# A gated recurrence followed by a highway layer: the identity taken from the raw w_h on GpSimd, w_t scaled on ScalarE, and a new hand-written order of the work

## The chip, the core and the metric

The kernel runs on one core of one Trainium2 chip. The metric is the device time of one execution in microseconds (us); the median of three executions of the kernel before is 207.73 us (207.66 to 208.34). The engines are PE (TensorE: transposes and matrix products), DVE (VectorE), ACT (ScalarE), POOL (GpSimd) and SP (SyncE, which issues the DMAs of this kernel).

## What is computed

`x` and `f_logit` are (4, 6336, 256) in float32, `lower_bound` has 256 entries, `w_h` and `w_t` are 256 by 256 and `b_t` has 256 entries.

```python
sig = 1 / (1 + exp(-f_logit))
f = lower_bound + (1 - lower_bound) * sig
i = 1 - f
for t in range(S):                       # each batch starts from h = 0
    h = f[:, t] * h + i[:, t] * x[:, t]
    y[:, t] = h
H = maximum(y @ w_h, 0)
T = 1 / (1 + exp(-(y @ w_t + b_t)))
out = T * H + (1 - T) * y
```

With c = 1 - lower_bound and u = sigmoid(-f_logit), f is 1 - c u and i is c u. The kernel leaves c out of the recurrence: it scans y' = f y' + u x, so y = c y', and puts c into the weights and into the diagonal that carries y to the output. Since out = y + T (max(y w_h, 0) - y), and max(a, 0) - y = max(a - y, -y), the kernel subtracts the identity from `w_h` once, and one DVE instruction gives the maximum.

## The kernel before

The 25344 tokens are cut into 21 units, listed in `parts` (line 42): units 0 and 1 have 2 blocks of 128 tokens, unit 2 has 4, units 3 to 6 and 14 to 18 have 8, units 7 to 13 have two halves of 8, units 19 and 20 have 4 and 2. A half is called a sub-unit.

The whole order is written out by hand as a string of tokens (lines 49 to 109). A loop at the end (line 414) reads the tokens one after another and calls the function of that letter; every instruction is pinned to that order on its engine, so each engine works through its own tokens in the order of the string and waits where an operand isn't there yet. A token is a letter, the unit, sometimes the sub-unit and a half, and after the colon the buffer or the PSUM banks. A trailing `v` puts the token on DVE instead of its usual engine.

The letters of one unit, in the order in which they depend on each other:

- `l`, `x` (SP, line 250): load f_logit and x. `u` (ACT, line 262): u = sigmoid(-l) in float16.
- `b`, `B` (POOL, or DVE with `v`, line 277): the product u x, as half a sub-unit (`b`) or a whole one (`B`). For 8 blocks `b` has 1024 elements in each partition, `B` 2048.
- `i`, `p` (PE, lines 286 and 311): transpose u and the product into PSUM, for feature half 0 or 1. `f` (ACT or DVE, lines 301 and 299): f from the transposed u.
- `s` (DVE, line 320): the recurrence along the tokens of one feature half. Each `s` of a unit starts from the last column of the unit before, so the scans of one feature half form a chain through the kernel.
- `z`, `g` (PE, lines 333 and 145): the two matrix products with `w_t` and `w_h`. `t` (ACT, line 356): the sigmoid of z. `d` (DVE, line 363): the maximum of g and -y. `e`, `E` (POOL or DVE, line 377): d times t, for one feature half or both.
- `o` (PE, lines 393 and 394): y times the diagonal plus the product, transposed back to tokens. `c` (ACT or DVE, lines 405 and 403): PSUM to SBUF. `w` (SP, line 411): the store.

`k*n` are n matrix products of zeros that nobody reads; there are 49 of them, all in the first part. Where DVE and POOL both multiply two SBUF tensors, the helper `shared` (line 193) makes the next POOL product wait for the last such DVE product.

Six tokens without a unit prepare constants. `wt` and `wh` (SP) load the two weights, `cc` (DVE) makes c, -c and the bias, `dg` (DVE, lines 219 and 220) a float16 diagonal of c and a float32 diagonal of -c, `WT` (DVE, line 224) scales w_t by c, and `WH` (DVE, lines 230 and 232) scales w_h by c and adds the negative diagonal to the two square blocks that hold the identity. All of them stand in the first 12 us.

Two queues set much of the order around the change. SP issues loads and stores in one line, and a store waits there for its `c`, so the loads behind it wait too. PE works through its tokens in one line as well; a `p` that waits for a product holds every later `z`, `g` and `o`.

Of the kernel before, what the change touches and what calls it, by code (L numbers as in the profile page):

```python
# [54 lines left out]
g2.0.0:1 d2.0.0:2 z2.0.0:0 t2.0.0:2 g2.0.1:3 k*1:2 o0.0.0:2 p3.0.1:0 l5.0:0 u4.0:0 z2.0.1:4 t2.0.1 e2.0.0 x5.0:0
b4.0.0:1 o1.0.0:1 p3.0.0:5 k*4:6 s3.1:0 l6.0:1 c0.0.0:0 x6.0:1 i4.0.1:4 f4.1:0 b4.0.1 k*4:0 k*4:0 s3.0:1 i4.0.0:0
l7.1:2 g3.0.1:67 d2.0.1 e2.0.1 c1.0.0v:1 w1.0.0 d3.0.1:3 u5.0:1 i5.0.1:2 p4.0.0:1 B5.0:2 i5.0.0:3 z3.0.0:45 f4.0:3
f5.1:2 f5.0:1 g3.0.0:67 z3.0.1:23 t3.0.0:0 w0.0.0 x7.1:2 s4.0:2 p4.0.1:0 p5.0.0:1 o2.0.0:45 u6.0:2 d3.0.0 e3.0.0
l7.0:3 t3.0.1 x7.0:3 c2.0.0:2 i6.0.1:6 f6.1:3 s4.1:3 g4.0.1:23 p5.0.1:0 u7.1:3 e3.0.1v d4.0.1:0 o3.0.1:45 c3.0.1:3
z4.0.1:67 t4.0.1:1 o3.0.0:23 z4.0.0:45 s5.0:4 i6.0.0:1 b6.0.1:0 c3.0.0:1 t4.0.0 g4.0.0:67 s5.1:5 g5.0.1:23 d4.0.0  # L60
b6.0.0 p6.0.0:0 z5.0.1:67 l8.0:4 f6.0:0 u7.0:0 t5.0.1:2 w3.0.1 l8.1:0 b7.1.1:1 x8.1:4 d5.0.1:1 z5.0.0:45 s6.0:0 t5.0.0
i7.0.1:23 i7.1.1 f7.1:1 b7.1.0 e4.0.1 e4.0.0v p6.0.1:1 s6.1:1 w2.0.0 g5.0.0:67 x8.0:0 o4.0.0:45 c4.0.0:0 g6.0.1:23
u8.0:1 l9.1:1 o4.0.1:45 p7.1.1:01 d5.0.0 b7.0.0:2 d6.0.1:2 c4.0.1:3 b7.0.1 p7.0.1 l9.0:2 e5.0.0v i7.0.0:67 e5.0.1
w3.0.0 u8.1:2 i7.1.0 s7.1:2 f7.0:2 p7.0.0:45 p7.1.0 z6.0.0:23 x9.0:1 z6.0.1:67 t6.0.0:0 t6.0.1 i8.0.1:01 s7.0:3 i8.1.1
i8.0.0:23 w4.0.0 g6.0.0:67 x9.1:2 d6.0.0 f8.1:0 i8.1.0 f8.0:3 o5.0.0:01 c5.0.0:2 g7.0.0:45 d7.0.0:3 u9.0:0 g7.1.1:23
d7.1.1:0 B8.1:0 p8.1.1:67 u9.1:3 g7.0.1:01 d7.0.1 o5.0.1:45 c5.0.1:1 B8.0:2 p8.0.1 s8.1:4 z7.0.1:23 t7.0.1:1 z7.1.1:01
w4.0.1 z7.0.0:45 t7.1.1:2 t7.0.0 p8.1.0:23 p8.0.0 E6.0 o6.0.1:01 c6.0.1:0 o6.0.0:67 c6.0.0:3 b9.0.0:1 z7.1.0:45
i9.0.0:01 b9.0.1 i9.1.0 b9.1.0:0 g7.1.0:67 t7.1.0 b9.1.1 l10.1:3 s8.0:5 l10.0:4 f9.0:1 i9.1.1:45 e7.0.1 u10.1:2 w5.0.1
d7.1.0 e7.0.0 g8.1.1:23 d8.1.1:1 x10.1:3 g8.1.0:01 d8.1.0 i9.0.1 f9.1:2 w5.0.0 g8.0.0:67 p9.1.1:23 p9.0.1 i10.1.0:01
# [111 lines left out]

# [270 lines left out]
```

## Time and profile before

| | us |
|---|---|
| median of three executions | 207.73 |
| the profiled execution | 208.83 |
| its span, first to last instruction | 207.1 |
| busy: PE, DVE, ACT, POOL | 194.7, 192.8, 190.9, 171.9 |
| first scan of unit 3 starts | 20.56 |
| first scan of unit 4 starts | 28.19 |
| last scan (unit 20) ends | 199.00 |
| last PSUM copy ends | 204.10 |

The profiled execution takes 1.73 us more than its span. The page lists for each engine how long it was busy; the views behind it list each instruction with its start, its duration, and in brackets the idle time of its engine before it with what ended that idle time. Durations of neighbours on DVE overlap a little: the start of the next lies some hundredths to a tenth of a microsecond before the end of the one before.

### The profile page before, as it was taken

To read this page: it belongs to the slowest core of one execution; us is meant where nothing else is said; L and a number is where in the kernel's file an instruction comes from. 1 tells how busy PE (TensorE), PEld (TensorE's weight loads), DVE (VectorE), ACT (ScalarE), POOL (GpSimd) and SP (SyncE) were. 2 spreads that over 40 slices of the span, in tenths; PEclk is the share of its full clock that TensorE was granted. 3 is DMA by queue.
4 is the path that set the end of the run, shared out by engine and by line. 5 is a ranking of instruction groups with operands and counts; after the bars stand their busy time and mean duration, and the time that the engine had idled before them with its cause. 6 is when DMAs were issued, how large, how long until landed. Compare 5 with 4: busy or idle time off the path is not lost.

```text
span 207.1 us, 4606 instructions
## 1 busy us (share of the span) xinstructions
PE 194.7 (94%) x1850; PEld 135.0 (65%) x1850; DVE 192.8 (93%) x141; ACT 190.9 (92%) x173; POOL 171.9 (83%) x90
## 2 busy tenths in 40 slices
PE   7999988998799999999989999999999999999991
PEld 2566657556566858747846967658767587677780
DVE  2799989999999999999999979999999999999971
ACT  4479699999999999999998999999999999998792
POOL 3173798978999999978998899979979949999920
PEclk9999999999999999999999999999999999999999
DMA  6999999999999999999999999999999999934576
GB/s 178 365 425 416 418 423 418 418 419 412 425 418 420 420 419 421 424 417 419 427 415 418 423 414 429 418 417 427 412 424 390 403 325 352 364 141 161 206 304 253
DMA packets 15980, 78.67 MB, mean 380 GB/s; under 512 B 1748, under 2 KB 2264, under 8 KB 10072
## 3 DMA queue, kind: packets, MB, share of 16 engines
q1 hardware_dynamic: 15952, 78.39, 93.5%
q8 instruction: 14, 0.23, 0.5%
q14 instruction: 6, 0.05, 0.1%
q10 hardware_dynamic: 8, 0.00, 0.0%
HBM read 52.43 MB, written 25.95 MB: 379 GB/s over the span
## 4 chain that ended last, share of the span: by engine, by line
PE 48%; DVE 17%; ACT 16%; DMA 11%; issue 4%; POOL 2%; SPq 1%; DVEq 0%; ACTq 0%
PE psum L333 13%; PE psum L145 11%; DMA l<-in_f_logit_dram 11%; DVE y L320 10%; PE psum L393 6%; DVE d L363 6%; PE psum L394 6%; ACT f L301 6%; PE psum L286 6%; PE psum L311 5%; ACT u L262 4%; ACT t L356 3%; ACT o L405 2%; POOL bv L277 2%; DVE f L299 1%
## 5 line engine op out<-in xcount | busy, mean ns | idle before, releaser
L277 POOL TENSOR_TENSOR bv<-u,x 128x1024 bf16<-128x1024 f16 (+2 forms) x44 | 99.8, 2293 | 18.3 <-ACT f L301 7.4
L320 DVE TENSOR_TENSOR_SCAN y<-f,y,psum 128x1024 bf16<-128x1024 f16 (+6 forms) x40 | 103.7, 2614 | 1.0 <-ACT f L301 0.6
L377 POOL TENSOR_TENSOR d<-d,t 128x1024 bf16<-128x1024 bf16 (+3 forms) x35 | 71.7, 2063 | 11.4 <-ACT t L356 6.1
L333 PE MATMUL psum<-y,w_sb 128*128 128x512 bf16 (+1 forms) x224 | 77.4, 367 | 3.0 <-ACT f L301 1.9
L145 PE MATMUL psum<-y,w_sb 128*128 128x512 bf16 x184 | 69.7, 379 | 0.7 <-DVE y L320 0.7
L363 DVE SCALAR_TENSOR_TENSOR d<-y,ncc,psum 128x1024 bf16<-128x1024 bf16 (+2 forms) x56 | 62.6, 1147 | 3.4 <-PE psum L145 1.5
L356 ACT ACTIVATE t<-psum,bt 128x1024 bf16<-128x1024 f32 (+2 forms) x56 | 56.3, 1038 | 2.6 <-PE psum L145 1.7
L262 ACT ACTIVATE u<-l 128x2048 f16<-128x2048 f32 (+2 forms) x28 | 48.6, 1747 | 5.4 <-DMA l<-in_f_logit_dram 5.4
L301 ACT ACTIVATE f<-psum,ncc 128x1024 f16<-128x1024 f16 (+3 forms) x38 | 50.9, 1365 | 1.6 <-PE psum L286 1.6
L405 ACT COPY o<-psum 128x1024 f32<-128x1024 f32 (+1 forms) x49 | 48.5, 1031 | 2.2 <-PE psum L394 1.0
L393 PE MATMUL psum<-diag,y 128*128 128x128 f16 x396 | 48.8, 219 | 0.6 <-ACT f L301 0.4
L394 PE MATMUL psum<-ident_b,d 128*128 128x128 bf16 x396 | 48.6, 219 | 0.8 <-DVE d L377 0.8
L394 PEld LDWEIGHTS <-d 128*128 128x128 bf16 x396 | 44.0, 113 | 4.8 <-DVE d L377 1.2
L393 PEld LDWEIGHTS <-y 128*128 128x128 bf16 x396 | 44.2, 113 | 2.5
L333 PEld LDWEIGHTS <-w_sb 128*128 128x128 f16 x224 | 21.6, 98 | 18.1 <-issue 1.0
L145 PEld LDWEIGHTS <-w_sb 128*128 128x128 f16 x184 | 17.9, 97 | 21.3 <-issue 6.0
L311 PE MATMUL psum<-ident_f,bv 128*128 128x128 f32 x198 | 29.3, 276 | 1.3 <-POOL bv L277 0.8
L286 PE MATMUL psum<-ident_h,u 128*128 128x128 f16 x396 | 28.6, 219 | 1.2 <-ACT u L262 0.8
L286 PEld LDWEIGHTS <-u 128*128 128x128 f16 x396 | 25.0, 98 | 6.9 <-ACT u L262 2.1
L311 PEld LDWEIGHTS psum<-ident_f,bv 128*128 128x128 f32 x198 | 22.4, 141 | 7.1 <-POOL bv L277 2.1
L377 DVE TENSOR_TENSOR d<-d,t 128x1024 bf16<-128x1024 bf16 (+3 forms) x15 | 10.6, 718 | 0.2
L145 PE MATMUL psum<-zeros 128*128 128x512 bf16 x39 | 10.6, 399 | 0.0
(33 smaller groups left out, 38.6 us busy)
## 6 DMA issues: line engine op xcount, KB each, us to landing
out_dram<-o SPq DMA_DIRECT2D x48, 512.0 KB, 7.9
l<-in_f_logit_dram SPq DMA_DIRECT2D x23, 1024.0 KB, 14.6
x<-in_x_dram SPq DMA_DIRECT2D x23, 1024.0 KB, 14.4
l<-in_f_logit_dram SPq DMA_DIRECT2D x2, 512.0 KB, 5.9
x<-in_x_dram SPq DMA_DIRECT2D x2, 512.0 KB, 7.4
l<-in_f_logit_dram SPq DMA_DIRECT2D x3, 256.0 KB, 3.7
x<-in_x_dram SPq DMA_DIRECT2D x3, 256.0 KB, 5.5
out_dram<-o SPq DMA_DIRECT2D x3, 256.0 KB, 5.6
```

The source lines that it names most:

```text
L145: return pe.add_instruction(mybir.InstMatmult(name=nc.get_next_instruction_name(), start_tensor_calc=start, stop_tensor_calc=stop, tile_si ...
L277: shared(pin(e.tensor_mul(st[n]["bv", s][:, a:c].rearrange("p k d j -> p k j d"), st[n]["u", s][:, 2 * a:2 * c].rearrange("p (k j) d -> p ...
L286: pin(nc.tensor.transpose(uT[:, j * P:(j + 1) * P], st[n]["u", s][:, j, h * P:(h + 1) * P], ident_h))
L301: pin(nc.scalar.activation(to, of, AF.Identity, scale=ncc[:, h:h + 1], bias=1.0))
L311: pin(nc.tensor.transpose(words[:, k:k + g * (P - 1) + 1:g], pair, ident_f))
L320: pin(nc.vector.tensor_tensor_scan(y[:, c:e], st[n]["f", h][:, c:e], data, 0.0 if fresh else carry[h], op0=ALU.mult, op1=ALU.add))
L333: pin(nc.tensor.matmul(p.part(a, e), w, data, start=ki == 0, stop=ki == NH - 1))
L356: pin(nc.scalar.activation(half(n, q, "t", m), z, AF.Sigmoid, bias=bt[:, m:m + 1]))
L363: pin(nc.vector.scalar_tensor_tensor(half(n, q, "d", m), y, ncc[:, m:m + 1], g, op0=ALU.mult, op1=ALU.max))
L377: shared(pin(e.tensor_mul(d, d, t)), not eng)
L393: pin(nc.tensor.matmul(o, st[n]["y", h][:, whole], diag[:, h], start=True, stop=False))
L394: pin(nc.tensor.matmul(o, half(n, q, "d", h)[:, cols], ident_b, start=False, stop=True))
```

## The change

There are two parts. The first concerns the constants. `WI`, a new token, subtracts the float32 identity from the two square blocks of the raw `w_h`, in place, on POOL. After it `WH` is two plain scalings on DVE (`WHv`), and `WT` becomes two scalings on ACT. `dg` makes only the diagonal of c; `ndiag` is gone. The constants' functions now take an engine.

```
-    ndiag = sb([P, NH, P], FP32, "ndiag")
...
-    def do_dg(slot):
+    def do_dg(slot, eng):
         for h in range(NH):
-            pin(nc.vector.tensor_scalar(diag[:, h], ident_h, cc[:, h:h + 1], None, op0=ALU.mult))
-            pin(nc.vector.tensor_scalar(ndiag[:, h], ident_h, ncc[:, h:h + 1], None, op0=ALU.mult))
-
-    def do_WT(slot):
+            if eng:
+                pin(nc.vector.tensor_scalar(diag[:, h], ident_h, cc[:, h:h + 1], None, op0=ALU.mult))
+            else:
+                pin(nc.gpsimd.tensor_scalar(diag[:, h], ident_h, cc[:, h:h + 1], None, op0=ALU.mult))
+
+    def do_WI(slot, eng):
+        e = nc.vector if eng else nc.gpsimd
         for h in range(NH):
-            pin(nc.vector.tensor_scalar(w_sb[:, 1, h], w_raw[:, 1, h], cc[:, h:h + 1], None, op0=ALU.mult))
-
-    def do_WH(slot):
+            own = w_raw[:, 0, h, h * P:(h + 1) * P]
+            shared(pin(e.tensor_tensor(own, own, ident_f, op=ALU.subtract)), not eng)
+
+    def scaled(k, eng):
         for h in range(NH):
-            own = slice(h * P, (h + 1) * P)
-            rest = slice((1 - h) * P, (2 - h) * P)
-            pin(nc.vector.scalar_tensor_tensor(w_sb[:, 0, h, own], w_raw[:, 0, h, own], cc[:, h:h + 1], ndiag[:, h],
-                                               op0=ALU.mult, op1=ALU.add))
-            pin(nc.vector.tensor_scalar(w_sb[:, 0, h, rest], w_raw[:, 0, h, rest], cc[:, h:h + 1], None,
-                                               op0=ALU.mult))
+            if eng:
+                pin(nc.vector.tensor_scalar(w_sb[:, k, h], w_raw[:, k, h], cc[:, h:h + 1], None, op0=ALU.mult))
+            else:
+                pin(nc.scalar.mul(w_sb[:, k, h], w_raw[:, k, h], cc[:, h:h + 1]))
+
+    def do_WT(slot, eng):
+        scaled(1, eng)
+
+    def do_WH(slot, eng):
+        scaled(0, eng)
```

The second part is the order: the whole string is replaced, and with it some choices of engine. Its first line before and after:

```
-l0.0:0 u0.0:0 pc:0 k*4:1 x0.0:0 b0.0.0v:0 p0.0.0:1 i0.0.1:2 cc dg f0.1v:0 p0.0.1:0 i0.0.0:3 l1.0:1 u1.0:1 l2.0:2
+pc:0 cc k*4:1 l1.0:0 l0.0:1 u1.0:0 u0.0:1 i0.0.0:0 x0.0:0 b0.0.0v:0 x1.0:1 b1.0.0v:1 i0.0.1:1 i1.0.1:2 f1.1:0 p0.0.0:3
```

Counted over the strings, the engine choices differ as follows. On DVE: `f` of a 2-block unit once instead of three times, half products `b` of 512 elements three times instead of once, `e` of 256, 512 and 1024 elements 4, 2 and 9 times instead of 1, 1 and 11, `E` of 2048 elements three times instead of twice, `c` of a full half twice instead of once. On POOL: `B` of 2048 elements 10 times instead of 4, and `b` of 1024 elements 25 times instead of 38. The number of matrix products is the same, with 49 of zeros in both. The loads of units 0 to 2 and of the weights stand in another order in SP's line; from `x2.0` to `l7.1` both strings have the same bytes ahead of each load.

DVE at the start of the program, from the first product to the scaling of w_h. Names are the tiles that an instruction writes and reads; `y<-` is a scan, `bv<-` a product, `w_sb<-` a scaled weight. Before:

```order
L277 TENSOR_TENSOR bv<-u,x 128x2x256
...
L219 TENSOR_SCALAR diag<-ident_h,cc 128x128
L220 TENSOR_SCALAR ndiag<-ident_h,ncc 128x128
L299 TENSOR_SCALAR f<-psum,ncc 128x256
L320 SCALAR_TENSOR_TENSOR y<-f,psum 128x256
L299 TENSOR_SCALAR f<-psum,ncc 128x256
L224 TENSOR_SCALAR w_sb<-w_raw,cc 128x256 x2
L320 SCALAR_TENSOR_TENSOR y<-f,psum 128x256
L230 SCALAR_TENSOR_TENSOR w_sb<-w_raw,cc,ndiag 128x128
L232 TENSOR_SCALAR w_sb<-w_raw,cc 128x128
...
L320 SCALAR_TENSOR_TENSOR y<-f,y,psum 128x256 x2
```

The same place now, down to the two scans of unit 2 (`y<-` of 128x512):

```order
L283 TENSOR_TENSOR bv<-u,x 128x2x256 x2
L305 TENSOR_SCALAR f<-psum,ncc 128x256
L218 TENSOR_SCALAR diag<-ident_h,cc 128x128 x2
L326 SCALAR_TENSOR_TENSOR y<-f,psum 128x256 x2
L326 SCALAR_TENSOR_TENSOR y<-f,y,psum 128x256
L231 TENSOR_SCALAR w_sb<-w_raw,cc 128x256 x2
L283 TENSOR_TENSOR bv<-u,x 128x2x256
L326 SCALAR_TENSOR_TENSOR y<-f,y,psum 128x256
L369 SCALAR_TENSOR_TENSOR d<-y,ncc,psum 128x256 x2
L383 TENSOR_TENSOR d<-d,t 128x256 x2
L369 SCALAR_TENSOR_TENSOR d<-y,ncc,psum 128x256
L326 SCALAR_TENSOR_TENSOR y<-f,y,psum 128x512 x2
```

The scaling of w_t and the negative diagonals are gone from DVE; two small products and two small `e` have come to it, and one scan of unit 1 stands ahead of the scaling of w_h.

ACT at the start, behind the loading of its table. `u` is the first sigmoid, `f` the factor of the recurrence, `t` the gate. Before:

```order
L262 ACTIVATE u<-l 128x512 x2
L262 ACTIVATE u<-l 128x1024
L301 ACTIVATE f<-psum,ncc 128x256 x2
L301 ACTIVATE f<-psum,ncc 128x512
L356 ACTIVATE t<-psum,bt 128x256 x2
```

Now:

```order
L268 ACTIVATE u<-l 128x512 x2
L307 ACTIVATE f<-psum,ncc 128x256 x2
L268 ACTIVATE u<-l 128x1024
L307 ACTIVATE f<-psum,ncc 128x256
L233 ACTIVATE w_sb<-w_raw,cc 128x256 x2
L307 ACTIVATE f<-psum,ncc 128x512
L362 ACTIVATE t<-psum,bt 128x256 x2
```

Two `f` have come ahead of the sigmoid of unit 2 (`u` of 128x1024), one `f` still stands behind it, and the scaling of w_t follows that.

POOL from unit 4 on, first before and then now. 128x2x2x256 is a half product, 128x4x2x256 a whole one.

```order
L377 TENSOR_TENSOR d<-d,t 128x512
L277 TENSOR_TENSOR bv<-u,x 128x2x2x256 x2
L377 TENSOR_TENSOR d<-d,t 128x512
L277 TENSOR_TENSOR bv<-u,x 128x4x2x256
L377 TENSOR_TENSOR d<-d,t 128x1024
L277 TENSOR_TENSOR bv<-u,x 128x2x2x256 x4
```

```order
L283 TENSOR_TENSOR bv<-u,x 128x4x2x256
L383 TENSOR_TENSOR d<-d,t 128x512
L283 TENSOR_TENSOR bv<-u,x 128x2x2x256 x2
L283 TENSOR_TENSOR bv<-u,x 128x4x2x256 x2
L383 TENSOR_TENSOR d<-d,t 128x1024 x2
```

The product of unit 4 is one whole instruction now, that of unit 5 two halves, and whole products follow where halves stood.

More of the change, by code (lines that the diff above doesn't have):

```diff
@@ L55 @@
[L55 to L69, printed above, removed]
@@ new lines @@
+b10.1.0 b10.0.0:2 l11.1:1 b10.0.1 e8.1.1 d9.0.0:3 u11.0:3 w7.0.0 g9.0.1:01 w6.0.0 d9.0.1 g8.0.1:45 d8.0.1 g9.1.1:67
+x11.0:0 i10.0.1:01 d9.1.1:0 x11.1:1 i10.1.1 c7.1.1:3 u11.1:1 p10.1.0:23 w7.0.1 l12.1:2 p10.0.0 w7.1.1 f10.1:2
+z9.0.1:45 t9.0.1:1 s10.0:2 z9.1.1:67 z9.0.0:01 E8.0 t9.1.1:2 t9.0.0 i11.0.1:45 i11.1.1 l12.0:3 p10.0.1:67 l13.1:4
+w7.1.0 B11.0:1 p10.1.1 b11.1.1:2 f11.1:0 x12.0:2 o8.1.0:01 c8.1.0:0 x12.1:3 s10.1:3 o8.1.1:23 c8.1.1:1 o8.0.1:45
+i11.0.0:01 c8.0.1:3 i11.1.0 f11.0:3 g9.1.0:23 g10.1.1:67 d9.1.0 d10.1.1:1 g10.1.0:45 d10.1.0 g10.0.1:23 b11.1.0
@@ L109 @@
+e20.0.1 g20.0.0:1 d20.0.0 w18.0.0 e20.0.0v o20.0.0:0 c20.0.0v:3 c19.0.0:0 w19.0.0 w20.0.0
 """
@@ L420 @@
         elif not name[1:2].isdigit():
-            here["do_" + name](slot)
+            here["do_" + name](slot, token.endswith("v"))
         else:
```

102 lines of the change are left out of this document (55 added, 47 removed).

## The prediction, made before the changed kernel had run

> **What bounds the kernel now.** I read the page first, for the engines' shares and the clock.
>
> ```profile
> span 207.1 us, 4606 instructions
> PE 194.7 (94%) x1850; PEld 135.0 (65%) x1850; DVE 192.8 (93%) x141; ACT 190.9 (92%) x173; POOL 171.9 (83%) x90
> PEclk9999999999999999999999999999999999999999
> ```
>
> Three engines are busy for over 90% of the span, so the shares alone don't name one. PE's share says least, since its matmuls are pipelined and their ends are modelled. The clock is full in every slice. The waits of DVE come next, then those of PE.
>
> ```profile
> DVE bv L277 <- ACT u L262: 3.1, 1, 3.1
> DVE d L363 <- PE psum L145: 1.5, 2, 1.2
> PE psum L333 <- ACT f L301: 1.9, 2, 1.3
> ```
>
> The columns are the total in us, the number of waits and the longest. DVE's list is short: one long wait at the start, and later next to nothing. PE's longest wait is 1.3 us, so idle time of TensorE costs here only what it makes others wait; the clock gives nothing back when it goes.
>
> The timeline shows where DVE's waits lie, and what paces the first 28 us.
>
> ```profile
> 8.08 1.06 ACT L262 ACTIVATE u<-l 128x1024 f16<-128x1024 f32 x1 [2.07 <-DMA l<-in_f_logit_dram]
> 20.56 4.58 DVE L320 TENSOR_TENSOR_SCAN y<-f,y,psum 128x1024 bf16<-128x1024 f16 x2 [0.26 <-PE psum L311]
> 22.65 4.25 POOL L277 TENSOR_TENSOR bv<-u,x 128x1024 bf16<-128x1024 f16 x2 [1.05 <-DMA x<-in_x_dram]
> 28.19 2.35 DVE L320 TENSOR_TENSOR_SCAN y<-f,y,psum 128x1024 bf16<-128x1024 f16 x1 [0.62 <-ACT f L301]
> 35.08 1.28 DVE L363 SCALAR_TENSOR_TENSOR d<-y,ncc,psum 128x1024 bf16<-128x1024 bf16 x1 [0.36 <-PE psum L145]
> 121.28 4.85 DVE L363 SCALAR_TENSOR_TENSOR d<-y,ncc,psum 128x1024 bf16<-128x1024 bf16 x4 [1.17 <-PE psum L145]
> 196.96 0.75 DVE L363 SCALAR_TENSOR_TENSOR d<-y,ncc,psum 128x512 bf16<-128x512 bf16 x1 [0.15 <-PE psum L333]
> 197.62 1.38 DVE L320 TENSOR_TENSOR_SCAN y<-f,y,psum 128x256 bf16<-128x256 f16 x2
> 201.93 0.48 DVE L363 SCALAR_TENSOR_TENSOR d<-y,ncc,psum 128x256 bf16<-128x256 bf16 x1 [1.06 <-ACT t L356]
> 203.51 0.59 ACT L405 COPY o<-psum 128x512 f32<-128x512 f32 x1 [0.76 <-ACT o L405]
> ```
>
> The kernel falls into three parts. Up to 28.19 us, the first scan of unit 4, DMA arrivals decide: ACT and POOL start when l and x land. From 28.19 to 199.00 (197.62 + 1.38), the end of the last scan, **DVE is the bound**: its listed waits there are 0.36 + 1.17 + 0.15 = 1.68 us in 170.8. The tail from 199.00 to the end is a chain of small steps. I sum the change over these three parts.
>
> **The change part by part.** The durations come from the groups with shapes kept apart (busy us, then mean ns of one).
>
> ```profile
> L377 DVE TENSOR_TENSOR d<-d,t 128x1024 bf16<-128x1024 bf16 x11 | 7.5, 695 | 0.0
> L277 DVE TENSOR_TENSOR bv<-u,x 128x2048 bf16<-128x2048 f16 x1 | 2.7, 2724 | 0.0
> L377 DVE TENSOR_TENSOR d<-d,t 128x2048 bf16<-128x2048 bf16 x2 | 2.4, 1208 | 0.0
> L299 DVE TENSOR_SCALAR f<-psum,ncc 128x256 f16<-128x256 f16 x3 | 1.4, 475 | 0.4 <-PE psum L286 0.3
> L403 DVE COPY o<-psum 128x1024 f32<-128x1024 f32 x1 | 1.2, 1197 | 0.0
> L230 DVE SCALAR_TENSOR_TENSOR w_sb<-w_raw,cc,ndiag 128x128 f16<-128x128 f32 x2 | 1.1, 531 | 0.2 <-DMA w_raw<-in_moe_w_h_dram 0.2
> L277 DVE TENSOR_TENSOR bv<-u,x 128x512 bf16<-128x512 f16 x1 | 0.7, 731 | 3.1 <-ACT u L262 3.1
> L224 DVE TENSOR_SCALAR w_sb<-w_raw,cc 128x256 f16<-128x256 f32 x2 | 0.6, 350 | 0.7 <-DMA w_raw<-in_moe_w_t_dram 0.7
> L220 DVE TENSOR_SCALAR ndiag<-ident_h,ncc 128x128 f32<-128x128 f16 x2 | 0.6, 280 | 0.0
> L232 DVE TENSOR_SCALAR w_sb<-w_raw,cc 128x128 f16<-128x128 f32 x2 | 0.5, 274 | 0.0
> L377 DVE TENSOR_TENSOR d<-d,t 128x512 bf16<-128x512 bf16 x1 | 0.4, 425 | 0.1
> L377 DVE TENSOR_TENSOR d<-d,t 128x256 bf16<-128x256 bf16 x1 | 0.3, 293 | 0.1
> L320 DVE TENSOR_TENSOR_SCAN y<-f,y,psum 128x256 bf16<-128x256 f16 x4 | 2.8, 728 | 0.0
> L363 DVE SCALAR_TENSOR_TENSOR d<-y,ncc,psum 128x256 bf16<-128x256 bf16 x6 | 2.7, 477 | 1.1 <-ACT t L356 1.1
> L356 ACT ACTIVATE t<-psum,bt 128x256 bf16<-128x256 f32 x6 | 2.5, 469 | 0.5 <-PE psum L333 0.5
> L262 ACT ACTIVATE u<-l 128x512 f16<-128x512 f32 x3 | 1.9, 629 | 1.9 <-DMA l<-in_f_logit_dram 1.9
> ```
>
> *DVE's work as a whole.* The weights take off 2 x 0.280 for the negative diagonals, 2 x 0.350 for w_t, and for w_h 2 x (0.531 + 0.274) less the 2 x 0.350 that `WHv` takes: 0.56 + 0.70 + 0.91 = 2.17 us. The new choices of engine add 2 x 0.731 (`b`), 3 x 0.293 + 0.425 - 2 x 0.695 + 1.208 (`e`, `E`) and 1.197 (`c`), and take 2 x 0.475 (`f`): 1.46 + 1.12 + 1.20 - 0.95 = 2.83. DVE ends up with 0.7 us **more** work. So the part of the change that is about the identity is worth nothing by itself; what counts is where the work lies.
>
> *Up to the first scan of unit 4.* `l2.0` stands 0.25 MB further back in SP's line. In these microseconds the DMAs move
>
> ```profile
> 5.00:10.00 5.00, 5.00 (x30) 2.57 (x29) 3.76 (x12) 2.41 (x4) 0.36 (x1) 1.00 0.93 353
> ```
>
> 353 GB/s (last column), so it lands 262144 B / 353 GB/s = 0.74 us later and `u2.0` starts at 8.82 instead of 8.08. It lasts 1.06; behind it on ACT stands `f1.0` (256 elements, like the 469 ns sigmoid), and DVE's third scan, `s1.0`, waits for that: it starts at 10.35, after a new wait of some 0.7 us, since all ahead of it on DVE is done by 9.6. Then DVE runs through: two scans of 0.728, `WHv` 0.70, a `b` of 0.731, three `d` of 0.477, two `e` of 0.293, the scans of unit 2 (5.0 for four of them in the trace, so 2.5), the product of unit 3 at 2.724, `d1.0.0` 0.477, two `d` of unit 2 (some 0.73 each), `e` of 0.425 and 0.293: 12.8 us, less 0.07 for each of 16 overlaps, 11.7. The first scan of unit 3 starts at 22.0 (20.56 before), and its pair of scans takes 4.58: 26.6. The next scan needs `B4.0`, one whole product on POOL now. Its x has the same bytes ahead of it, so it starts at 22.65 as before, lasts about two halves (4.25), ends at 26.9 and is transposed in some 0.5: **unit 4's first scan starts at 27.4, 0.8 earlier** than at 28.19, where it waited for ACT. Bounds: 26.6, if the product comes in time, and 28.6, if ACT's new work is late. That work, two scalings of 256 by float32, lies by the two ACT rows between 2 x 0.469 and 2 x 0.629; it falls behind `u2.0`, where ACT otherwise waits for l3.0 until 13.97, and is hidden; without that cover it costs 0.9 to 1.3. `WI` on POOL (two of 128 elements, between nothing and the 0.7 of a product of 512 on DVE) falls into a stretch in which POOL was idle until 9.63.
>
> *From there to the end of the last scan.* Between these two scans the strings differ on DVE by one `c` (+1.20), one `d` of 1024 that used to be done earlier (+1.27, by the row at 35.08), one `E` for two `e` (+1.21 - 1.39) and one `f` (-0.48): **+1.81 us**. Against it stand the 1.68 us of waits, which belong to the old order. If the new one has none, this part takes 170.8 - 1.68 + 1.81 = 170.9 us; every wait that it has adds its length. Between none and the 1.7 of the old order, I take 0.1, as near to none as the stretch from 36 to 120 us, in which DVE did not wait at all.
> The loads move too. The one that I find closest is unit 9's last x: 1 MB more stands ahead of it than ahead of unit 9's last x before.
>
> ```profile
> 60.00:80.00 20.00, 19.72 (x190) 13.63 (x188) 20.00 (x12) 19.82 (x15) 20.00 (x9) 1.00 1.02 420
> 66.05 8.46 POOL L277 TENSOR_TENSOR bv<-u,x 128x1024 bf16<-128x1024 f16 x4
> 78.78 8.84 DVE L320 TENSOR_TENSOR_SCAN y<-f,y,psum 128x2048 bf16<-128x2048 f16 x2
> ```
>
> Before, the third of these four products read it at 70.3. At 420 GB/s 1 MB is 2.5 us, so it lands by 72.8; the whole product ends by 77.1 and is transposed by 77.8, 1 us ahead of the scan at 78.78. That load is hidden; if a store holds SP's line by more than that 1 us, DVE waits for the rest. ACT has one copy less here, POOL fewer products in fewer instructions, and both have room; PE has the same instructions.
>
> *The tail.* The steps from the last scan to the last copy are the same in both strings, `c20` on DVE apart, which saves a handover at most. I take 0 (-0.3 to +0.5).
>
> The sum is -0.8 + 1.81 - 1.68 + 0.1 = -0.6, rounded to -0.7 for the waits under 0.3 us in the old order that no list shows. The profiled execution's 208.83 (its span and 1.73 around it) would become 208.1; the median of the three shown is 1.10 lower, and 207.73 - 0.7 is **207.0 us**.
>
> **A resource that the sum leaves out.** DVE and POOL are not independent when both read two SBUF tensors.
>
> ```profile
> 32.03 2.14 POOL L377 TENSOR_TENSOR d<-d,t 128x1024 bf16<-128x1024 bf16 x1
> 33.88 0.84 DVE L377 TENSOR_TENSOR d<-d,t 128x1024 bf16<-128x1024 bf16 x1
> 45.77 0.67 DVE L377 TENSOR_TENSOR d<-d,t 128x1024 bf16<-128x1024 bf16 x1
> ```
>
> The `e` at 33.88 starts while a POOL product runs until 34.17 and takes 0.84 us; the one at 45.77, with POOL idle, takes 0.67. The old order has its DVE products where POOL stands still or is about to end, so the trace shows only a few tenths lost; it does not show a DVE product that meets a POOL product at its start. The Trainium skill, page "SBUF — State Buffer", section "Who interferes with whom", says that a DVE instruction with two SBUF inputs and a GpSimd instruction that reads SBUF exclude each other for the whole instruction, and that the first to issue wins. By that rule a DVE product can lose a whole POOL product, by the two rows alone a few tenths; the rule speaks against this change, which has longer products on POOL. The 0.84 us agrees with it.
>
> **The rivals.** *One old-sized wait.* The new order keeps DVE as dense as the old one, but has its own wait like that of 1.17 us at 121.28, behind PE. For it: the one order that the trace shows has such a wait, and PE's line is as full as before. Then the sum is +0.5: 208.2 us. Waits between 0.3 and 1.5 us belong here.
>
> *DVE meets the longer POOL products.* POOL has 15 instructions of 2048 elements instead of 8, and they take about 4.25 us. DVE has 3 `E` and 9 full `e` to place between them. Where it arrives in the middle of one, it waits for half on average, 2.1 us; from two such places on, with only one of them at full length, the kernel is slower: 207.0 + 2.1 = 209.1, and 211 for two. It decides once POOL runs more than 0.7 us ahead or behind of the plan at an `E`, for then the gain is gone. Against it: POOL has fewer products in all, so it waits more often than DVE does, and the DVE products stand in fewer clusters.
>
> *The front does more than I think.* If `B4.0` comes in time, the scan starts at 26.6, and with a clean middle the time is 206.2.
>
> **How the numbers follow.** Less than 0.3% of this kernel, 0.6 us, can't be told from no change. My forecast, a clean middle and 206.5 to 207.2, has 0.37, of which 0.33 is faster by more than that. The front that does more has 0.07, all faster. The old-sized wait, 207.2 to 208.4, has 0.23, the longer POOL products, 208.4 to 211, have 0.33. The forecast's part above 207.1 (0.04) and all but 0.01 of the old-sized wait count as no change. So faster has 0.40, same 0.26, slower 0.34. The range from 206.0 to 210.0 leaves out some 0.04 below and 0.15 above. The forecast's own range is 206.2 to 207.3.
>
> **What would show it.** Right: unit 4's first scan near 27.4 with a wait for PE's transposes before it; a wait of about 0.7 us before DVE's third scan; no wait of DVE above 0.3 us between 30 and 195 us; DVE busy for about 193.5 us. Wrong: the same total of waits in the middle under other names (the first rival), or DVE products of `d<-d,t` far above 0.7 us for 1024 elements, or POOL starting just before them (the second). A granted clock below 1.0 anywhere would overturn the sum altogether.

## The result, and the profile after

The changed kernel takes **210.03 us** (median of seven executions, 209.46 to 213.91), the kernel before beside it 208.16 (seven, 207.66 to 208.57): a ratio of 1.0092, 95% interval 1.0065 to 1.0120. A second set gave 209.85 us and 1.0071 (1.0046 to 1.0097). In each of the two sets one execution (213.91 and 212.76 us) was disturbed and is left out of the ratio. So the change makes the kernel slower by 0.5 to 1.2%. The prediction of 207.0 us was wrong, and its range, up to 210.0, ends just short of the first median.

The page of the profiled execution (209.70 us):

```profile
span 207.9 us, 4595 instructions
PE 194.5 (94%) x1850; PEld 134.9 (65%) x1850; DVE 193.1 (93%) x139; ACT 191.8 (92%) x176; POOL 166.7 (80%) x80
```

The sums are those of before to 1 us, POOL apart. The timeline of DVE, with the rows that stand where the prediction put its steps:

```profile
10.42 0.75 DVE L326 TENSOR_TENSOR_SCAN y<-f,y,psum 128x256 bf16<-128x256 f16 x1 [1.39 <-ACT f L307]
26.90 2.35 DVE L326 TENSOR_TENSOR_SCAN y<-f,y,psum 128x1024 bf16<-128x1024 f16 x1 [0.64 <-PE psum L317]
172.27 9.09 DVE L326 TENSOR_TENSOR_SCAN y<-f,y,psum 128x1024 bf16<-128x1024 f16 x4
182.11 3.66 DVE L369 SCALAR_TENSOR_TENSOR d<-y,ncc,psum 128x1024 bf16<-128x1024 bf16 x3 [0.75 <-PE psum L144]
192.58 1.28 DVE L369 SCALAR_TENSOR_TENSOR d<-y,ncc,psum 128x1024 bf16<-128x1024 bf16 x1 [0.54 <-PE psum L144]
199.41 0.74 DVE L326 TENSOR_TENSOR_SCAN y<-f,y,psum 128x256 bf16<-128x256 f16 x1
204.27 0.69 DVE L409 COPY o<-psum 128x512 f32<-128x512 f32 x1 [0.66 <-PE psum L400]
```

The front came: unit 4's first scan starts at 26.90 instead of 28.19. Unit 16's first scan starts at 172.27, and before it was 172.41; the lead is nearly gone by then. The last copy ends at 204.96 instead of 204.10, so about 1 us is lost behind unit 16's first scan, where two waits of DVE for PE (0.75 and 0.54) are new. I cut the time at these two scans, in us:

| trace | unit 4's first scan starts | from there to unit 16's | from there to the end of the last copy |
|---|---|---|---|
| before, and a second trace of it | 28.19, 27.90 | 144.22, 144.05 | 31.69, 31.69 |
| changed, and a second trace of it | 26.90, 26.96 | 145.37, 145.23 | 32.70, 32.39 |

The profiled executions are 0.9 us apart, the medians 1.5 to 1.9: the profiled one of before, at 208.83, lies above its median of 208.16 (the second trace of it has a span of 206.6 us, not 207.1), and those of the changed kernel, at 209.70 and 209.31, lie below theirs.

What holds PE in the last part is on ACT's list of waits, and before it had no such entry:

```profile
ACT o L411 <- DMA out_dram<-o: 1.7, 4, 0.8
```

Copies wait for stores. The chain that ended last shows one o buffer go round:

```profile
157.03 1.03 ACT o L411
158.08 7.49 DMA out_dram<-o
165.67 1.02 ACT o L411
166.71 9.38 DMA out_dram<-o
176.18 1.02 ACT o L411
```

The columns are start and length. c12.0.0 fills the buffer, its store takes 7.49 us, then c13.1.1 may fill it, that store takes 9.38, and then c14.0.0. The timeline around the last step:

```profile
165.75 0.38 SPq L256 DMA_DIRECT2D x<-in_x_dram  x1
166.71 7.46 SPq L417 DMA_DIRECT2D out_dram<-o  x3
176.18 1.01 ACT L411 COPY o<-psum 128x1024 f32<-128x1024 f32 x1 [0.83 <-DMA out_dram<-o]
177.25 0.38 PE L339 MATMUL psum<-y,w_sb 128*128 128x512 bf16 x1 [0.58 <-ACT o L411]
```

SP issued a 1 MB load (x18.0) at 165.75 and the store behind it at 166.71. The copy c14.0.0 waits 0.83 us for that store, PE's z15.0.1 waits 0.58 for the bank that c14.0.0 frees, and DVE's d16.0.0 waits 0.75 for PE, at 182.11.

### The profile page after: what moved, and what is told of

It is laid out like the page before. It is cut to its first block, busy times and chain, and to the rows that moved or that the text cites. A ratio compares the mean times of both kernels' runs of the same rounds, so it can differ in the third digit from the quotient of the medians.

```text
span 207.9 us, 4595 instructions
## 1 busy us (share of the span) xinstructions
PE 194.5 (94%) x1850; PEld 134.9 (65%) x1850; DVE 193.1 (93%) x139; ACT 191.8 (92%) x176; POOL 166.7 (80%) x80
## 4 chain that ended last, share of the span: by engine, by line
PE 44%; DMA 16%; POOL 14%; issue 10%; ACT 8%; DVE 5%; SPq 1%; ACTq 0%; POOLq 0%; DVEq 0%
PE psum L339 12%; DMA out_dram<-o 12%; POOL bv L283 11%; PE psum L144 10%; PE psum L399 6%; PE psum L317 6%; PE psum L400 6%; PE psum L292 4%; DMA x<-in_x_dram 4%; POOL d L383 3%; ACT o L411 3%; DVE y L326 2%; ACT f L307 2%; ACT u L268 2%; ACT t L362 2%
## 5 line engine op out<-in xcount | busy, mean ns | idle before, releaser
L283 POOL TENSOR_TENSOR bv<-u,x 128x1024 bf16<-128x1024 f16 (+2 forms) x37 | 97.0, 2641 | 17.3 <-PE psum L292 6.3
L383 POOL TENSOR_TENSOR d<-d,t 128x1024 bf16<-128x1024 bf16 (+3 forms) x30 | 68.7, 2303 | 10.8 <-DVE d L383 4.3
L307 ACT ACTIVATE f<-psum,ncc 128x1024 f16<-128x1024 f16 (+3 forms) x40 | 51.6, 1307 | 2.1 <-PE psum L292 1.5
L411 ACT COPY o<-psum 128x1024 f32<-128x1024 f32 (+1 forms) x48 | 47.7, 1019 | 3.9 <-DMA out_dram<-o 1.7
L383 DVE TENSOR_TENSOR d<-d,t 128x1024 bf16<-128x1024 bf16 (+3 forms) x18 | 11.4, 654 | 0.4
L326 DVE TENSOR_TENSOR_SCAN y<-f,psum 128x256 bf16<-128x256 f16 (+3 forms) x8 | 10.0, 1266 | 0.1
```

The costliest lines, as they stand in the source:

```text
L283: shared(pin(e.tensor_mul(st[n]["bv", s][:, a:c].rearrange("p k d j -> p k j d"), st[n]["u", s][:, 2 * a:2 * c].rearrange("p (k j) d -> p ...
L307: pin(nc.scalar.activation(to, of, AF.Identity, scale=ncc[:, h:h + 1], bias=1.0))
L326: pin(nc.vector.tensor_tensor_scan(y[:, c:e], st[n]["f", h][:, c:e], data, 0.0 if fresh else carry[h], op0=ALU.mult, op1=ALU.add))
L383: shared(pin(e.tensor_mul(d, d, t)), not eng)
```

## The experiments

All ratios are to the kernel before on the same chip. The interval is that of 95%.

| kernel | ratio | interval |
|---|---|---|
| constants alone, in the old order | 1.0087 | 1.0058 to 1.0117 |
| the same, POOL's product held back | 1.0003 | 0.9979 to 1.0028 |
| changed, again | 1.0071 | 1.0046 to 1.0097 |
| changed, five o buffers in turn | 1.1033 | 1.0992 to 1.1075 |
| changed, two stores earlier | 1.0098 | 1.0066 to 1.0131 |
| changed, fifth buffer for one copy | 1.0051 | 1.0024 to 1.0078 |
| and two products exchanged | 1.0298 | 1.0253 to 1.0343 |
| and a third product earlier | 1.0065 | 1.0042 to 1.0088 |
| changed, l16.0 earlier | 1.0064 | 1.0044 to 1.0085 |
| changed, a copy back on ACT | 1.0125 | 1.0098 to 1.0152 |
| changed, l16.0, the copy, the buffer | 1.0072 | 1.0046 to 1.0099 |
| changed, all cures for stores and lock | 1.0003 | 0.9977 to 1.0029 |
| before, again | 1.0000 | 0.9972 to 1.0028 |
| before, g9.0.1 (PE) twice | 1.0048 | 1.0030 to 1.0066 |
| before, d9.0.1 (DVE) twice | 1.0071 | 1.0044 to 1.0097 |
| before, t9.0.1 (ACT) twice | 1.0032 | 1.0014 to 1.0050 |
| before, g14.0.1 (PE) twice | 1.0029 | 1.0008 to 1.0050 |
| before, d14.0.1 (DVE) twice | 1.0082 | 1.0050 to 1.0114 |

### The constants alone

The old order with the new constants:

```
-... cc dg f0.1v:0 ...   wt WT ...   wh WH ...
+... cc dgv f0.1v:0 ...  wt WT ...   wh WI WHv ...
```

> The first part of the change alone: the identity subtracted from the raw w_h on POOL, w_t scaled on ACT, no negative diagonals, in the order of the kernel before, with its buffers and engines otherwise. DVE has 2.2 us less work, all of it in the first 12 us. My prediction's view (the first 28 us follow DMA arrivals, so DVE's work there is hidden): 0.997 to 1.003 of the kernel before. Rival (DVE is bound from its first product on, so that its work counts in full): 0.990. A third way: ACT's or POOL's new instructions, which are not hidden in the old order, delay f or the products of the first units: 1.002 to 1.006.

It took 1.0087, above all three, though its interval, from 1.0058, still touches the third. DVE's timeline, then POOL's:

```profile
11.14 2.67 DVE L232 TENSOR_SCALAR w_sb<-w_raw,cc 128x256 f16<-128x256 f32 x2 [2.50 <-POOL w_raw L227]
```

```profile
11.49 2.18 POOL L284 TENSOR_TENSOR bv<-u,x 128x1024 bf16<-128x1024 f16 x1
```

Two scalings of 0.35 us take 2.67: the second starts at 11.60, in the first tenth of a POOL product, and ends at 13.82, just behind it (11.49 + 2.18 = 13.67). So I held the product back behind the scaling:

```
-                pin(nc.vector.tensor_scalar(w_sb[:, k, h], ...))
+                shared(pin(nc.vector.tensor_scalar(w_sb[:, k, h], ...)), False)
```

> The constants' part alone in the old order, as in the run that took 1.0087, with one more dependency: POOL's product of unit 2 waits for DVE's scaling of w_h. In that run the second scaling started at 11.60, 0.11 us after this product, and ended at 13.82, 0.15 us after it: 2.22 us instead of 0.35. Theory L (a lock between DVE and POOL, for the length of the instruction that came first): each scaling takes about 0.35 us, the scans of unit 1 start near 11.8 instead of 13.74, the first scan of unit 3 near 20.8 instead of 22.63, and the time is 0.998 to 1.003 of the kernel before. Rival (the loss is in the later w_h or in ACT's scaling of w_t, and the long record only shows it): the scans of unit 1 stay near 13.7 and the time near 1.009.

DVE, then POOL:

```profile
12.10 0.79 DVE L232 TENSOR_SCALAR w_sb<-w_raw,cc 128x256 f16<-128x256 f32 x2 [3.77 <-POOL w_raw L227]
```

```profile
13.02 2.14 POOL L284 TENSOR_TENSOR bv<-u,x 128x1024 bf16<-128x1024 f16 x1 [0.55 <-DVE w_sb L232]
```

The two scalings take 0.79 us and the time is 1.0003. In this execution POOL's subtraction came 0.95 us later than in the run before, so the scans of unit 1 start at 12.81 and not near 11.8. Theory L holds, and the constants are worth nothing when the two don't meet. The Trainium skill, page "SBUF — State Buffer", section "Who interferes with whom", also names `tensor_scalar`, which can run in a mode that takes both ports of DVE, as one that GpSimd can block for a whole instruction; the 2.22 us of this scaling, which reads one SBUF tensor, agree.

### The late stretch of the changed kernel

The base was measured again:

> The changed kernel once more, as the base for the runs beside it and for a second trace of it. Expected: about 1.009 of the kernel before (1.006 to 1.012). In its trace the front should repeat (first scan of unit 4 near 26.9, last scan's end near 200.2). If the late waits of DVE for PE's d banks (0.75 us before d16.0.0, 0.54 before d18.0.1) are set by the order or by stores, they come again within some 0.3 us; if they were an accident of one execution, they don't.

The waits before d16.0.0 (0.45 us) and d18.0.1 (0.54) came again.

**Stores moved** in SP's line:

```
-... c12.1.1:3 i15.0.0:2 ...  x18.0:1 c13.1.1:0 ... w13.1.1 o13.0.1:23 ... l19.0:2 w12.1.1
+... c12.1.1:3 w12.1.1 i15.0.0:2 ...  c13.1.1:0 ... w13.1.1 x18.0:1 o13.0.1:23 ... l19.0:2
```

> The changed kernel with two tokens moved in SP's line alone: the store w13.1.1 ahead of the load x18.0 (1 MB) instead of behind it, and w12.1.1 right behind its copy instead of behind l19.0. No compute engine's order changes. Theory S: the store lands some 2 to 3 us earlier, ACT's wait of 0.83 us before c14.0.0 goes, and DVE's 0.75 us before d16.0.0 with it: 0.5 to 0.8 us faster than the changed kernel beside it, near 1.006 of the kernel before. It could also move the wait to x18.0, which then lands about as much later. Theory P: no difference, 1.009.

The waits of c14.0.0 and of d16.0.0 are gone, as theory S has it, and the time is no better. The later load came back as a wait of POOL for x; DVE shows what that did:

```profile
176.34 2.15 POOL L283 TENSOR_TENSOR bv<-u,x 128x1024 bf16<-128x1024 f16 x1 [1.86 <-DMA x<-in_x_dram]
182.62 4.23 POOL L383 TENSOR_TENSOR d<-d,t 128x1024 bf16<-128x1024 bf16 x2
```

```profile
185.24 2.16 DVE L383 TENSOR_TENSOR d<-d,t 128x1024 bf16<-128x1024 bf16 x1
```

e16.0.1 on DVE arrives at 185.24 inside POOL's second product, which ends at 182.62 + 4.23 = 186.85, and takes 2.16 us instead of 0.69. In both traces of the changed kernel the same pair missed each other by 0.01 us: POOL ended at 185.68 and 185.30, DVE began at 185.69 and 185.31. The margin repeats because the end of d16.0.0 starts both: POOL's product e16.0.0 needs it and ends 3.57 us after d16.0.0's start, and DVE gets to e16.0.1 after 3.58 us. They meet when POOL comes to e16.0.0 late; here its product before, e15.0.1, ends only at 184.76, long behind d16.0.0.

**A fifth buffer.** First all copies in turn over five (36 tokens have another buffer):

> The changed kernel with five o buffers instead of four, used in turn. A copy then waits for the store five copies back instead of some four back. Theory S (ACT's copies wait for stores that stand behind 1 MB loads, PE then waits for the banks that the copies free, and DVE for PE): the waits of ACT for stores (0.83 us before c14.0.0, 0.33 and 0.37 before two copies of unit 13) go, and with them most of the 0.75 + 0.54 us of DVE's late waits; 0.7 to 1.3 us faster than the changed kernel beside it, 1.003 to 1.006 of the kernel before. Theory P (the late waits are the line of PE itself, full as it is, and the stores only show up beside it): ACT's waits for stores go, DVE's late waits and the time stay, 1.009.

```profile
ACT o L411 <- DMA out_dram<-o: 19.7, 4, 9.5
```

A badly made experiment: in that order a copy gets a buffer whose store stands far back in SP's line, and ACT waits 19.7 us. The time (230.49 us) is 20.6 us above the changed kernel's. TensorE's granted clock fell as well, to 0.95 on the average of this trace, so not all of that need be the waits themselves. It tells only that these waits are not hidden.

Then one copy alone, `c13.1.1:4` for `c13.1.1:0`:

> The changed kernel with a fifth o buffer that only c13.1.1 uses (c13.1.1:4 for c13.1.1:0); nothing else is moved, SP's line neither. Theory S (the late wait of DVE comes from a store): ACT's waits before c13.1.1 (0.37 us) and c14.0.0 (0.83, 0.53 in the second trace) go, and DVE's wait before d16.0.0 (0.75, 0.45) with them. How much of that the end gains is where two forms of S part. Without a lock between DVE and POOL: the whole 0.45 to 0.75 us. With it: d17.0.0 ends earlier by that much, so that the product e16.0.1 on DVE arrives while POOL's e16.0.0 still runs; it is then recorded with 1.0 to 1.3 us instead of 0.69 and the end gains only 0.1 to 0.4. Theory P (PE's own line): d16.0.0 waits as before, no gain.

ACT, then DVE:

```profile
178.16 1.01 ACT L411 COPY o<-psum 128x1024 f32<-128x1024 f32 x1 [0.94 <-DMA out_dram<-o]
```

```profile
182.17 3.66 DVE L369 SCALAR_TENSOR_TENSOR d<-y,ncc,psum 128x1024 bf16<-128x1024 bf16 x3 [0.80 <-PE psum L144]
185.75 1.04 DVE L383 TENSOR_TENSOR d<-d,t 128x1024 bf16<-128x1024 bf16 x1
```

The wait went over to the next copy, c14.0.1, which waits for the store of c13.1.0, and the lock took 0.35 us more. In this trace ACT also waited 1.40 us for a load (until 155.89; in the two traces of the changed kernel 0 and 0.4 us). Its ratio can't be told from that of the changed kernel. To keep the lock out I exchanged two products, twice:

```
-... d16.0.1 ... d17.0.0:3 ... e15.0.1 ... e16.0.0 ... e16.0.1v
+... d16.0.1 e16.0.0v ... d17.0.0:3 ... e15.0.1 ... e16.0.1        (first)
+... d16.0.1 e15.0.1 e16.0.0v ... d17.0.0:3 ... e16.0.1            (second)
```

> The kernel of the run before with one exchange in addition: the first half product of unit 16 (e16.0.0) on DVE, right behind d16.0.1 and ahead of d17.0.0, and the second (e16.0.1) on POOL behind it, so that DVE's product can't arrive in the middle of a POOL product. DVE and POOL have the same work as before. With the lock: DVE's product takes 0.69 us, the end gains the whole 0.45 to 0.75 us against the changed kernel, 1.004 to 1.007 of the kernel before, and the spread from run to run gets smaller, if it comes from such meetings. Without a lock: the same as the run before. If o16.0.0 on PE then waits for the POOL half (it ends near 186.5 instead of 185.7), up to 0.5 us is lost again.

> The run that took 1.030 (fifth o buffer for c13.1.1, e16.0.0 on DVE ahead of e16.0.1 on POOL), with e15.0.1 ahead of e16.0.0 in the string as well. There the helper's dependency had caught e15.0.1 as the next POOL product, which then waited 3.34 us for DVE, PE's o15.0.0 4.6 us for it and the scans of unit 18 4.16 us for PE. If that was all, the time falls to that of the fifth buffer alone or a little below: 1.002 to 1.006. If not, it stays above 1.01. In the run with the fifth buffer alone the wait for a store had only gone over to c14.0.1 (0.94 us), d16.0.0 waited 0.80 us as before, and e16.0.1 on DVE took 1.04 us; the last can't happen here: 0.3 us.

POOL and DVE in the first:

```profile
186.00 4.21 POOL L383 TENSOR_TENSOR d<-d,t 128x1024 bf16<-128x1024 bf16 x2 [3.33 <-DVE d L383]
```

```profile
191.27 2.35 DVE L326 TENSOR_TENSOR_SCAN y<-f,y,psum 128x1024 bf16<-128x1024 f16 x1 [4.16 <-PE psum L400]
```

The dependency that avoids the lock held the wrong product, e15.0.1. With that one ahead, the time is 1.0065, d16.0.0 waits 0.15 us, no product is held, and the last part takes 32.08 us instead of 32.39 and 32.70. That is theory S for the last part alone: the part before it takes 145.73 us instead of 145.23 and 145.37, so that the gain is gone in the sum (177.81 us, between 177.62 and 178.07), and the ratio shows none.

**A load moved.** `l16.0:1` from behind `w11.1.1` to right behind `x15.0:3`:

> The changed kernel with one load moved in SP's line: l16.0 (1 MB) right behind x15.0, so ahead of the store w11.1.1, which holds SP from 137.4 to 144.7 us until its copy is done. Theory M (in the changed order too few bytes stand queued when SP stops there, the DMAs run short, 349 and 327 GB/s from 145 to 155 us against 411 and 425 before, some 0.9 MB or 2 us of transfer are lost, and all later stores and loads land late): these two stretches come back to 400 to 425 GB/s, ACT's waits for stores between 160 and 180 us (1.5 us in all) and POOL's waits for x there go, DVE's wait before d16.0.0 shrinks; 0.5 to 1.3 us faster than the changed kernel, 1.001 to 1.006 of the kernel before. Rival P (PE's line sets d16.0.0): the stores come earlier, the time stays at 1.007 to 1.009.

The windows of the changed kernel, of the one before, and of this one; the last column is GB/s, the one ahead of it the DMAs' busy share:

```profile
145.00:150.00 5.00, 5.00 (x40) 3.06 (x39) 5.00 (x4) 5.00 (x5) 5.00 (x4) 1.00 1.01 349
150.00:155.00 5.00, 5.00 (x39) 3.00 (x38) 4.92 (x4) 4.94 (x5) 5.00 (x3) 1.00 0.97 327
```

```profile
145.00:150.00 5.00, 5.00 (x56) 3.50 (x54) 5.00 (x4) 5.00 (x5) 5.00 (x3) 1.00 1.00 411
150.00:155.00 5.00, 4.89 (x43) 2.97 (x42) 4.93 (x6) 4.98 (x6) 3.46 (x3) 1.00 1.03 425
```

```profile
145.00:150.00 5.00, 5.00 (x40) 3.29 (x39) 4.93 (x5) 5.00 (x6) 5.00 (x4) 1.00 1.01 416
150.00:155.00 5.00, 5.00 (x38) 2.79 (x37) 4.96 (x4) 4.91 (x5) 5.00 (x3) 1.00 1.03 424
```

Theory M holds for the transfers, and unit 16's first scan starts at 171.16, 1.1 us earlier (0.4 of it by an earlier start of unit 4, at 26.50). It does not hold for ACT's waits, nor for the time (1.0064):

```profile
175.66 1.01 ACT L411 COPY o<-psum 128x1024 f32<-128x1024 f32 x1 [1.79 <-DMA out_dram<-o]
```

c14.0.0 waits 1.79 us for the same store as before, and the last part takes 33.28 us.

**A copy moved** to ACT, `c11.0.1:3` for `c11.0.1v:3`:

> The changed kernel with the copy c11.0.1 (1.22 us, at 148.9) back on ACT; DVE has one copy of a full half left, as before the change. Theory D (DVE is the bound of the middle, so that the work that came to it counts in full): 1.2 us faster than the changed kernel, near 1.002 of the kernel before. Rival A (ACT, without any gap over 0.1 us from 127 to 164 us in the changed kernel, is as full as DVE and sets the middle with it): between no gain and 1 us slower, 1.007 to 1.012, with new waits of DVE for f or of PE for t behind 150 us.

```profile
150.28 2.60 DVE L369 SCALAR_TENSOR_TENSOR d<-y,ncc,psum 128x1024 bf16<-128x1024 bf16 x2 [1.20 <-POOL d L383]
```

Theory D falls here. Where the copy stood, DVE now waits 1.20 us for a POOL product: the copy had filled a hole. And the time rises by about what ACT got: 1.0125 against 1.0071 is 1.1 us, the copy 1.02. With the load, the copy and the buffer together:

> The three together: l16.0 ahead of w11.1.1, c11.0.1 on ACT, and the fifth o buffer for c13.1.1. If M and D both hold, 1.7 to 2.5 us faster than the changed kernel: 0.997 to 1.001 of the kernel before. If only M holds: as the run with l16.0 alone, 1.001 to 1.006. If neither: 1.006 to 1.010.

It took 1.0072, as the changed kernel. But beside the copy alone (1.0125) that is 1.1 us less, so the load and the buffer together gave back here what neither gave by itself; the two intervals (up to 1.0099, from 1.0098) barely overlap. This trace still has a product of DVE inside one of POOL's: e16.0.1 took 1.04 us.

**All cures at once**, with the copy left on DVE:

```
-x15.0:3 ... l16.0:1 | c12.1.1:3 ... w12.1.1 | c13.1.1:0 | c14.0.1:1 | d16.0.1 ... e15.0.1 ... e16.0.0 ... e16.0.1v
+x15.0:3 l16.0:1 ... | c12.1.1:3 w12.1.1 ... | c13.1.1:4 | c14.0.1:3 | d16.0.1 e15.0.1 e16.0.0v ... e16.0.1
```

> The changed kernel with all the small cures at once, and c11.0.1 left on DVE: l16.0 ahead of w11.1.1 in SP's line, w12.1.1 right behind its copy, five o buffers (c13.1.1 in the fifth, c14.0.1 in that of c12.1.1), e16.0.0 on DVE ahead of e16.0.1 on POOL. No copy of units 13 and 14 then waits for a store that lands late. Theory S in its whole form (all that the changed order loses behind 160 us hangs on these stores and on the one lock): ACT's waits for stores and PE's gaps between 160 and 180 us (0.95 us) go, 0.8 to 1.3 us faster than the changed kernel, 1.001 to 1.004 of the kernel before. Rival (ACT's and PE's lines are full there and take the place of the stores): 1.005 to 1.007, as each cure by itself.

ACT's waits from 155 to 185 us, then DVE's timeline:

```profile
ACT o L411 <- PE psum L400: 1.3, 1, 1.3
ACT o L411 <- DMA out_dram<-o: 0.2, 1, 0.2
```

```profile
180.41 2.44 DVE L369 SCALAR_TENSOR_TENSOR d<-y,ncc,psum 128x1024 bf16<-128x1024 bf16 x2
184.91 4.58 DVE L326 TENSOR_TENSOR_SCAN y<-f,y,psum 128x1024 bf16<-128x1024 f16 x2 [0.18 <-PE psum L400]
191.31 1.28 DVE L369 SCALAR_TENSOR_TENSOR d<-y,ncc,psum 128x1024 bf16<-128x1024 bf16 x1 [0.64 <-PE psum L400]
```

208.58 us, 1.0003. d16.0.0, at 180.41, doesn't wait any more. By the ratios that is 0.7 to 0.9% below the changed kernel, and the intervals (up to 1.0029, and from 1.0046) don't meet. So the cures together give the loss back by the ratio, and no single one can be told from the changed kernel: as one wait goes, the next link of copy, store, bank and product takes its place.

The trace is more sober. Its parts are 26.50 (0.4 us less than in the changed kernel, by the arrival of the first loads), 144.94 and 32.26 us. From unit 4's first scan to the end of the last copy that is 177.20 us, against 178.07 and 177.62 in the changed kernel and 175.90 and 175.74 before. The cures shorten this stretch by 0.4 to 0.9 us, and it stays 1.4 us longer than before; the earlier start of unit 4 pays for that. What stays is DVE's work: up to the last scan DVE is busy for 170.45 us here and for 168.63 before, and its idle time, 1.9 us, is below the 2.2 of before. So the stores, with the lock beside them, are a part of what the changed order loses behind its front. It doesn't beat the kernel before; no version here does.

### What a microsecond costs

The kernel before again, and with one instruction written twice in the string (the second writes the same result), in the same place otherwise:

> The kernel before once more, for a second trace of it beside the others. Its first trace has a span of 207.1 us, the longer half of its runs (205.9 to 207.7, the middle one 206.6), so a typical one should be some 0.5 us shorter. If the difference lies in the first 28 us, in the arrival of loads, the first scan of unit 4 starts earlier than 28.19 and all behind it is alike; if it is spread over the middle, it isn't to be had by the order of the front.

> The kernel before with one pair of w_h products done twice (g9.0.1, near 92 us; 1.03 us of PE more, the same result). The prediction's view (DVE alone bounds the middle; PE's line is full by its modelled ends, but follows): 1.000 to 1.001. The other view (PE, DVE and ACT bind each other, so that a microsecond more on any of them shows): up to 1.005. PE's gaps between 80 and 120 us were 1.0 us together.

> The kernel before with one maximum done twice (d9.0.1, near 94 us; 1.27 us of DVE more, the same result). DVE alone as the bound of the middle: 1.27 us slower, 1.006. If it is given back where DVE waits later for PE (1.17 us at 121): 1.000 to 1.002.

> The kernel before with one gate done twice (t9.0.1, near 97 us; 1.13 us of ACT more, the same result), for ACT what the runs with g9.0.1 and d9.0.1 were for PE (1.0048 for 1.03 us) and DVE (1.0071 for 1.27 us). If ACT binds there as they do: 1.004 to 1.006. If it has room: 1.000 to 1.002. ACT's gaps from 60 to 120 us were 0.9 us together.

> The kernel before with g14.0.1 done twice (near 164 us; 1.03 us of PE more, the same result). There PE had gaps of 0.14 us in all from 140 to 200 us. Theory PE (PE sets the last 40 us, so a wait of PE there, as those behind the copies c14 in the changed order, costs its whole length): 1.0 us slower, 1.005. The prediction's view (DVE sets it): 1.000 to 1.001.

> The kernel before with d14.0.1 done twice (near 165 us; 1.27 us of DVE more, the same result). Theory PE: less than half of it shows, 1.000 to 1.003, since DVE runs ahead of PE there. The prediction's view: 1.27 us slower, 1.006. Both engines without slack (each waits for the other within a few microseconds): 1.005 to 1.006 here and in the run with PE's product.

From unit 4's first scan to the end of the last copy, which leaves the arrival of the first loads out, the two traces of before have 175.90 and 175.74 us. The differences to their mean follow; by its 95% interval, each ratio's time is uncertain by 0.4 to 0.7 us:

| doubled | its length | time, by the ratio x 208.4 us | time, by the trace |
|---|---|---|---|
| PE near 92 us | 1.03 | 1.00 | 0.87 |
| DVE near 94 us | 1.27 | 1.48 | 1.40 |
| ACT near 97 us | 1.13 | 0.67 | 0.54 |
| PE near 164 us | 1.03 | 0.60 | 0.99 |
| DVE near 165 us | 1.27 | 1.71 | 1.11 |

DVE's work counts in full, as the prediction had it. But PE's counts nearly as fully (0.6 to 1.0 us for 1.03), and ACT's by about half. No theory with a single bound holds. In the trace of the doubled d9.0.1,

```profile
92.59 3.78 DVE L363 SCALAR_TENSOR_TENSOR d<-y,ncc,psum 128x1024 bf16<-128x1024 bf16 x3
```

stands where two such instructions took 2.46 us, and the 1.17 us of DVE's wait at 121 did not take it up.

## Why the prediction was wrong

*The constants: right, with a condition it did not name.* They are worth nothing by themselves, but in the old order only once POOL's product is held off DVE's scaling. In the new order `WHv` (0.59 us) meets none.

*The front: right in the main, the size short.* Forecast 27.4, measured 26.90 and 26.96, a gain of 1.29 instead of 0.8. As forecast, POOL's `B4.0` sets it: in all eleven traces with this front unit 4's first scan starts 4.9 us behind it. But `B4.0` came at 21.99 and 22.05, not 22.65. Its x landed at 21.67 and 21.89 (before at 22.49, and in the second trace of before at 21.85, so the forecast had started from a late landing). In the first of the two traces `B4.0` starts 0.23 us behind a small product of DVE (ends 21.76) for which the helper `shared` makes it wait, a dependency that the forecast left out. That `s1.0` came at 10.42 (forecast 10.35) is chance: the second trace has it at 9.43, and unit 4's scan no earlier for that.

*DVE's work: right.* 193.1 us (193.5 forecast).

***The step that failed* is the term of the waits in the middle:** "Between none and the 1.7 of the old order, I take 0.1". The changed kernel's waits there, from unit 4's first scan to the end of the last scan, add up to 2.5 us with the small ones: 0.75 and 0.54 behind PE, and 1.2 in ten waits of 0.05 to 0.23. The old order's are 2.1 counted in the same way. So the +1.81 us of work stands without the 1.68 against it: this part became 2.44 us longer (173.25 and 170.81), where I had 0.2. DVE's busy time in it rose by 1.98 us, from 168.63 to 170.61, near the forecast; its idle time rose by 0.46, where the sum took 1.58 off. Cut at unit 16's first scan, the idle time did fall ahead of it, from 1.99 to 1.24 us, and rose behind it, from 0.19 to 1.40. Why the small waits are there is not shown. Front, middle and tail are -1.29 + 2.44 - 0.29 = +0.86, the difference of the two traces.

*What stood behind that step was wrong too:* "ACT has one copy less here, POOL fewer products in fewer instructions, and both have room; PE has the same instructions." The windows, busy us of PE, PEld, DVE, ACT and POOL, before and after, say otherwise:

```profile
160.00:180.00 20.00, 19.97 (x203) 14.31 (x201) 19.90 (x13) 20.00 (x21) 17.06 (x7) 1.00 0.95 355
180.00:200.00 20.00, 20.00 (x212) 14.74 (x210) 19.56 (x17) 17.66 (x20) 17.37 (x9) 1.00 0.53 207
```

```profile
160.00:180.00 20.00, 19.05 (x210) 14.41 (x209) 19.80 (x13) 18.47 (x19) 16.20 (x9) 1.00 0.95 347
180.00:200.00 20.00, 20.00 (x194) 13.81 (x193) 18.60 (x16) 17.69 (x22) 15.46 (x9) 1.00 0.58 229
```

Before, PE, DVE and ACT were all three full from 160 to 180 us; these rows could have been read before the run. After, PE stands idle for 0.95 us there. If a wait of PE costs what a doubled product costs in that place, 0.6 to 1.0 for each microsecond, this alone would be most of the late loss of 0.7 to 1.0 us; that is an estimate.

*The transfers.* I asked of one load, x9.0, whether a store could hold it, and it was not late. I did not ask it of the stores: when they land, and which copy waits for the buffer. That is where it happened, behind x18.0.

*The rivals.* The first, "one old-sized wait" behind PE, was right in kind, with two waits in place of one, so that its 208.2 us was too low. The second, DVE held by a POOL product, did not happen in either trace of the changed kernel (685 ns per product of 1024, 695 before), but it is real: 2.16 us in one variant, 1.04 in two others, 2.22 in the constants alone. That some executions of the changed kernel have such a meeting, with 0.01 us between the two in both traces, would fit, but no trace shows it. The third had the front nearly right (26.6, and 26.90 came), but not the clean middle that it needs as well.

*The clock* was 1.00 in all rows of the changed kernel up to 200 us.

What stays open: how that which the cures together give back (1.4 to 1.9 us by the ratios, 0.4 to 0.9 by the traces behind the front) divides among them, and why the medians lie further apart than the traces.

## What to carry to other kernels

When three engines are full in the same window, the one with the fewest waits need not be "the bound": write one instruction of each twice, and see what a microsecond costs, before work is moved between them. For each buffer that a store empties, add the store's landing time, with the loads queued ahead of it, to the time at which the next copy wants the buffer. Where two engines can lock each other out, a wait that is taken away upstream can move one into the other, so a cure has to come with the order of the two fixed.
